# Attention scores as pairs of 64-row fp32 matmuls, reciprocals shared by two steps, and a new order

## The chip, the cores and the metric

The kernel runs on one core of one Trainium2 chip. The metric is device time in microseconds of one execution. The profile is that of one execution of the kernel before; all its times count from the start of its span.

## The reference

Attention over 4 batches of 8 heads, 576 tokens, 64 values a head. Only probabilities near the maximum are kept. Two feed-forward layers follow on 2304 tokens of 512 values, with 2048 hidden values each. Everything is float32.

```python
def _attn_ref(q, k, v, tau):
    scores = 1.0 / np.sqrt(q.shape[-1]) * np.matmul(q, k.transpose(0, 1, 3, 2))
    thresh = np.max(scores, axis=-1, keepdims=True) - tau
    scores = np.where(scores >= thresh, scores, -1000000000.0)
    attn = np.exp(scores - np.max(scores, axis=-1, keepdims=True))
    attn = attn / (np.sum(attn, axis=-1, keepdims=True) + 1e-09)
    return np.matmul(attn, v)

def _moe_ref(x, w_in, w_out):          # the second layer has max(0.01 * h, h) in place of g
    h = x @ w_in
    r = np.maximum(h, 0.0)
    g = r * r
    return g @ w_out
```

## The kernel before

**Attention.** The 32 heads are 16 pairs, four pairs to a batch, and each pair has nine steps (`steps`, `step`): four blocks of 128 query rows for each of its two heads, and one step of the 64 rows left over of both heads. 144 steps in all. A step computes 128 x 576 scores into the tile `s` (two PSUM banks of 288 columns each, index `g`; there are two such tiles), then on VectorE (DVE) the negated row maximum `nb` (L539), on ScalarE (ACT) `e`, the exponential (L540), a threshold `th` of 128x1 on DVE or GpSimd (POOL, L541 and L542), on DVE the masked `e` with its row sum (L544), then `t` and the reciprocal `r` of 128x1 (L547, L549). `e` times `r` is turned round and multiplied with the values.

**Two ways for the scores** (`prep` loads for one, `qk` at L529 multiplies). Pairs 0 to 5 (`nat`) keep queries and keys in fp32: the tile `Q` has one head's 64 rows and 64 rows of zeros, `KH` holds the keys of both heads one below the other, and each bank is one fp32 matmul over 128 rows. An fp32 matmul stands in the trace as two records. Pairs 6 to 15 split: queries and keys are rounded to fp32r on ACT, and the rests come from subtractions on POOL or DVE; `Q` holds the query's high part above its low part, `KH` and `KL` the two parts of the keys, and each bank takes two fp32r matmuls (`KH`, `KL`), the leftover step four. The leftover step of pairs 0 to 5 has products of 64 output columns that lie side by side in the array (the trace shows them as 128*64).

**Turning and values.** Pairs 0 to 4 (`nav`) turn `e` on TensorE (PE) through a unit matrix (L565, L566), copy it on ACT, and multiply in fp32 with 64 output columns at a time (`av32`, L631). Later pairs write `e` in two fp16 parts, turn them by DMA, and multiply in fp16 (L627); the last products of each group have 64 columns. `xs` adds the halves (L644 on DVE) and a DMA writes it to DRAM (`x1d`).

**Feed-forward.** While attention runs, the first layer works on the first 1792 tokens in seven blocks of 256, with 12 of the 16 weight blocks (`ffn`, `NFA`; h at L675, y at L701, all in fp32r parts, three products each). When attention is over, the other four weight blocks, the last 512 tokens and the second layer follow in blocks of 512 (h at L811, y at L857). Weights come as 512 KB loads that DVE, ACT and POOL unpack and split (`w_block`, L349 to L354).

**What sets the order.** `Plan.order` writes out every engine's order before the program is built: each operation has a priority (its step plus an offset from `CFG`), a cost, engines that may do it with a price for each, and tiles in rings of a fixed number of buffers. Engines then run their lists in that order, so a late instruction holds all behind it on its engine.

## Time and profile before

| | |
|---|---|
| time, median of 3 runs (lowest to highest) | 1092.0 us (1087.91 to 1092.18) |
| the profiled execution: time, and span of its trace | 1087.9 us, 1086.1 us |
| PE busy | 1059.4 us (98%) |
| DVE, ACT, POOL busy | 732.8 (67%), 509.1 (47%), 342.1 us (31%) |
| granted TensorE clock | full in each of 40 slices |
| HBM read and written | 70.98 and 17.83 MB |

The shares of the whole span mix three stages: attention alone at the start, attention with the first layer between its steps, and feed-forward alone at the end. Matmuls are pipelined, so that a PE that is busy throughout can still lose time between matmuls; starts of successive matmuls tell more than the busy time. POOL's times are rough.

### The profile page before, as it was taken

The page shows a single profiled execution, that of the slowest core. Times are in us where ns is not written, and L with a number is a line of the kernel's source. Part 1 is how long each engine was busy: PE and PEld are TensorE (multiplying, and loading weights), DVE is VectorE, ACT ScalarE, POOL GpSimd, SP SyncE. Part 2 cuts the span into 40 slices and gives each one's busy share as a digit, 9 for nine tenths or more (in the row PEclk, how much of TensorE's full clock was granted, in tenths as well). Part 3 has the DMA queues.
Part 4 walks back from the last instruction along what each step waited for, and adds up shares of the span by engine and source line. Part 5 has one row for each costly group of instructions (what it writes and reads, how often), then busy time and mean ns, then how long its engine had stood idle before and what let it go on. Part 6 is the DMA issues. An engine that isn't in the chain of part 4 may idle for free.

```text
span 1086.1 us, 17711 instructions
## 1 busy us (share of the span) xinstructions
PE 1059.4 (98%) x6343; PEld 886.1 (82%) x6343; DVE 732.8 (67%) x1557; ACT 509.1 (47%) x902; POOL 342.1 (31%) x421
## 2 busy tenths in 40 slices
PE   8988999999999999999999999999999999999998
PEld 4555778888998889989888888888888888888887
DVE  7999898788988898756999975763423433433343
ACT  6899878876776788735343431221211111111121
POOL 5765778889886676410000000000000000000000
PEclk9999999999999999999999999999999999999999
DMA  7444449998888896745644543610100100010010
GB/s 196 122 133 144 137 108 193 181 171 171 169 171 149 172 169 119 142 83 180 227 138 155 181 147 123 225 41 0 70 8 1 39 20 1 1 40 1 1 40 20
DMA packets 186983, 119.16 MB, mean 110 GB/s; under 512 B 146064, under 2 KB 164624, under 8 KB 186896
## 3 DMA queue, kind: packets, MB, share of 16 engines
q1 hardware_dynamic: 186528, 117.82, 44.3%
q8 instruction: 50, 0.82, 0.3%
q10 hardware_dynamic: 368, 0.21, 0.1%
q14 instruction: 37, 0.30, 0.1%
HBM read 70.98 MB, written 17.83 MB: 82 GB/s over the span
## 4 chain that ended last, share of the span: by engine, by line
PE 65%; DVE 1%; ACT 1%; issue 0%; POOL 0%; ACTq 0%; POOLq 0%; DVEq 0%
PE h L811 26%; PE y L857 26%; PE h L675 5%; PE y L701 5%; PE o L627 2%; PE s L529 2%; DVE e L544 0%; DVE nb L539 0%; DVE P L308 0%; ACT e L540 0%; ACT P L554 0%; DVE gl L308 0%; DVE P L587 0%; ACT tmp L639 0%; POOL t L547 0%
## 5 line engine op out<-in xcount | busy, mean ns | idle before, releaser
L823 DVE TENSOR_TENSOR r<-h,r 128x512 f32<-128x512 f32 (+1 forms) x80 | 51.0, 638 | 211.4 <-ACT r L822 211.4
L822 ACT ACTIVATE r<-h 128x512 f32<-128x512 f32 (+1 forms) x80 | 44.5, 557 | 313.1 <-PE h L811 310.6
L310 POOL TENSOR_TENSOR xl<-xr,xh 128x512 fp32r<-128x512 f32 (+1 forms) x11 | 12.7, 1157 | 418.3 <-ACT xh L297 253.5
L544 DVE SCALAR_TENSOR_TENSOR e<-s,th,e 128x576 f32<-128x576 f32 x144 | 116.8, 814 | 31.5 <-ACT e L540 27.4
L529 PE MATMUL s<-KH,Q 128*128 128x288 f32 (+1 forms) x440 | 121.1, 368 | 10.1 <-DVE e L544 6.6
L540 ACT ACTIVATE e<-s,nb 128x576 f32<-128x576 f32 x144 | 106.7, 742 | 38.5 <-DVE nb L539 22.5
L539 DVE TENSOR_REDUCE nb<-s 128x1 f32<-128x576 f32 x144 | 107.8, 750 | 12.4 <-PE s L529 11.3
L529 PEld LDWEIGHTS s<-KH,Q 128*128 128x128 f32 (+1 forms) x440 | 73.6, 183 | 30.6 <-issue 12.3
L308 DVE TENSOR_TENSOR gl<-r,gh 128x512 fp32r<-128x512 f32 (+1 forms) x129 | 85.6, 664 | 8.2
L587 DVE SCALAR_TENSOR_TENSOR P<-e,r,P 128x576 f16<-128x576 f32 x59 | 57.1, 970 | 2.8 <-ACT P L554 1.7
L819 ACT ACTIVATE r<-h 128x512 f32<-128x512 f32 (+1 forms) x32 | 18.2, 573 | 86.4 <-PE h L811 80.1
L627 PE MATMUL o<-PT,VA 128*128 128x320 f16 (+1 forms) x396 | 56.5, 287 | 0.4 <-DVE xs L644 0.4
L529 PE MATMUL s<-KL,Q 128*128 128x288 f32 x200 | 55.8, 294 | 0.0
L299 DVE CAST gh<-r 128x512 fp32r<-128x512 f32 (+1 forms) x103 | 43.8, 425 | 15.9 <-ACT r L684 7.8
L310 POOL TENSOR_TENSOR gl<-r,gh 128x512 fp32r<-128x512 f32 (+1 forms) x25 | 32.7, 1309 | 58.7 <-issue 45.2
L352 DVE SCALAR_TENSOR_TENSOR wraw<-wraw 128x512 int32<-128x512 int32 x64 | 48.9, 765 | 1.7 <-ACT wraw L349 0.6
L349 ACT ACTIVATE wraw<-wraw 128x512 f32<-128x512 f32 x64 | 43.0, 681 | 9.9 <-DMA wraw<-w 9.7
L354 DVE SCALAR_TENSOR_TENSOR wraw<-wraw 128x512 int32<-128x512 int32 x64 | 45.9, 717 | 0.6
L542 POOL TENSOR_SCALAR th<-nb,ca 128x1 f32<-128x1 f32 x75 | 33.3, 444 | 37.0 <-DVE nb L539 29.3
L627 PEld LDWEIGHTS <-VA 128*128 128x128 bf16 x396 | 35.2, 98 | 10.8 <-issue 0.4
L554 ACT ACTIVATE e<-e,r 128x576 f32<-128x576 f32 x51 | 39.4, 776 | 7.5 <-DVE r L549 6.9
L310 POOL TENSOR_TENSOR P<-e,P 128x576 f16<-128x576 f32 x29 | 38.7, 1339 | 8.5 <-ACT P L297 7.6
(616 smaller groups left out, 3044.5 us busy)
## 6 DMA issues: line engine op xcount, KB each, us to landing
wraw<-w SPq DMA_DIRECT2D x64, 512.0 KB, 4.1
wraw<-qT SPq DMA_DIRECT2D x20, 288.0 KB, 4.2
wraw<-kT SPq DMA_DIRECT2D x20, 288.0 KB, 4.4
out<-yo SPq DMA_DIRECT2D x18, 256.0 KB, 2.0
VA<-vv SPq DMA_DIRECT2D x32, 128.0 KB, 2.8
x2d<-yo SPq DMA_DIRECT2D x16, 256.0 KB, 3.3
xr<-x2d SPq DMA_DIRECT2D x4, 1024.0 KB, 5.8
y1d<-ys SPq DMA_DIRECT2D x14, 256.0 KB, 2.8
```

The lines of the kernel that those rows point to most:

```text
L308: alts.append(("V", dve(n), lambda: nc.vector.tensor_tensor(out=o(), in0=a(), in1=b(), op=alu), kind + "*"))
L310: alts.append(("G", pool2(n), lambda: nc.gpsimd.tensor_tensor(out=o(), in0=a(), in1=b(), op=alu), kind))
L529: nc.tensor.matmul(ps.get()[r, g, 0:S2], lhsT=o.Q.get()[:, q], rhs=(kk.get() if o.KL else f32(kk.get()))[:, g_(g)], start=k == 0 or not o. ...
L539: op(("V", 0.75, lambda: nc.vector.tensor_reduce(out=nb.get(), in_=pv(), axis=AX.XY, op=ALU.max, negate=True)), [ps], [nb], i + CFG["pd1"] ...
L540: op(("A", 0.74, lambda: nc.scalar.activation(e.get(), pv(), AF.Exp, bias=nb.get(), scale=1.0)), [ps, nb], [e], i + CFG["pex"], True)
L544: op(("V", 0.82, lambda: nc.vector.scalar_tensor_tensor(out=e.get(), in0=pv(), scalar=th.get(), in1=e.get(), op0=ALU.is_ge, op1=ALU.mult, ...
L587: op(("V", 0.8, lambda: nc.vector.scalar_tensor_tensor(out=lo(), in0=ev(), scalar=r_.get(), in1=hi(), op0=ALU.mult, op1=ALU.subtract), "*" ...
L627: nc.tensor.matmul(ps.get()[r, c_], lhsT=f_(v), rhs=parts16(pt)[:, j, c_], start=(k == 0), stop=k >= len(prods) - 2)
L675: nc.tensor.matmul(ps.get()[:, i], lhsT=a.get()[:, kc * P:(kc + 1) * P], rhs=x.get()[:, kc], start=(i == 0 and q == 0 and kc == 0), stop=( ...
L701: nc.tensor.matmul(yp[m // 2].get()[:, m % 2], lhsT=a.get()[:, c], rhs=x.get()[:, i], start=(f + i == 0 and q == 0 and m % 2 == 0), stop=( ...
L811: nc.tensor.matmul(ps.get()[:, 0:n], lhsT=a.get()[:, kc * P:(kc + 1) * P], rhs=x.get()[:, kc, 0:n], start=(q == 0 and kc == 0), stop=(q == ...
L857: nc.tensor.matmul(o(), lhsT=l, rhs=r, start=(first and q == 0), stop=(last and q == 2))
```

## The change

All 16 pairs compute their scores in one way. `Q` and `K` hold both heads' values in fp32 on partitions 0 to 63, and on partitions 64 to 127 the same queries again, with the other half of the keys' columns. A step is two fp32 matmuls over 64 rows each, one in the upper and one in the lower half of the array, each to a bank of its own; the leftover step has four of 64 rows and 64 columns. The splitting of queries and keys and the zero fill are gone. The heads of a pair take turns in the order of steps. The sums of two successive steps share one tile of two columns, with one `t` and one reciprocal for both; `th` is a subtraction. Some work may run on other engines (weights on POOL, two more `xs`), rings have other sizes, and all costs and offsets of the planner are new. Tokens 512 to 1023 do only 10 of the 12 weight blocks during attention (`nf`), and the two others afterwards.

```diff
-    lead1=1.311, xsg0=[1], lbm=8, lb=[[0, 1, 3, 4, 7], [0, 1, 3, 7], [3, 5], [2, 3, 5, 7]], xsm=4, xsg=[], dq=1.2, xu=False, pqk=-3.705,
...
+    hor=0.226, xlead=6.455, eb=5, pb=4, ptb=4, qb=2, nav=5, vb=2, tmb=1, gb=2, xb=1, w2step=-2.023, nf=[12, 10, 12, 12], wo=0.676, slack=0,
...
-    head, tail = [(0, 0), (0, 1), (1, 0), (1, 1)], [(0, 2), (0, 3), (None, MAIN), (1, 2), (1, 3)]
+    what = [(0, 0), (1, 0), (0, 1), (1, 1), (0, 2), (1, 2), (None, MAIN), (0, 3), (1, 3)]
...
+        Q, K = o.Q, o.K = [val("att", r, CFG["qb"], [P, 2, c], F32) for r, c in (("Q", S), ("K", S2))]
+        for g in range(2):
+            rows = slice(g * D, (g + 1) * D)
+            dma(lambda g=g, rows=rows: K.get()[rows], lambda g=g: kT[b, h0:h0 + 2, :, g * S2:(g + 1) * S2].rearrange("h d s -> d h s"), [], [K], at(0) if n else -3.1, D * S * 4, urgent=n == 0)
+            dma(lambda rows=rows: Q.get()[rows], lambda: qT[b, h0:h0 + 2].rearrange("h d s -> d h s"), [], [Q], at(0) if n else -3.05, 2 * D * S * 4, q=nc.sync if n else nc.scalar, urgent=n == 0, issue=0.5 if n else 0.06)
+        op(times(K.get, S)[0:None if n else 1], [K], [K], at(1))
...
+                    if h is None:
+                        a, q, r = j, slice((1 - j) * MAIN * P, (1 - j) * MAIN * P + REM), slice(j * REM, (j + 1) * REM)
+                    elif j == 0:
+                        a, q, r = h, slice(h * REM + t * P, h * REM + (t + 1) * P), slice(0, P)
...
+                    nc.tensor.matmul(ps.get()[r, g, 0:S2], lhsT=o.Q.get()[rows(g), a, q], rhs=o.K.get()[rows(g), a], start=True, stop=True)
...
+        k = i % 2
+        if not k:
+            sums[:] = [val("small", r, 3, [P, 2], F32) for r in ("sum", "t", "r")] + [Val(), Val()]
...
+        if k:
+            op([(g, c_, lambda eng=eng: eng.tensor_scalar(out=t_.get(), in0=sm.get(), scalar1=1e-9, scalar2=1.0 / UP, op0=ALU.add, op1=ALU.mult), "t")
+                for g, c_, eng in (("V", 0.148, nc.vector), ("G", 0.192, nc.gpsimd))], sums[0:1] + sums[3:], [t_], i + CFG["pd2"], True)
+            op(("V", 0.16, lambda: nc.vector.reciprocal(out=r_.get(), in_=t_.get())), [t_], [r_], i + CFG["pd2"], True)
```

Three places of the new order follow. In each row the line is that of its own kernel, then the operation, and the tiles (written <- read) with the size. The first place is PE in the middle of attention, between blocks of the first layer (h is L675 before and L635 now). Before:

```order
L675 MATMUL h<-xh,w8ih 128x256 x4
L675 MATMUL h<-xl,w8ih 128x256 x4
L675 MATMUL h<-xh,w8il 128x256 x4
L529 MATMUL s<-KH,Q_3644 128x288
L529 MATMUL s<-KL,Q_3644 128x288
L529 MATMUL s<-KH,Q_3644 128x288
L529 MATMUL s<-KL,Q_3644 128x288
```

Now:

```order
L635 MATMUL h<-xh,w8ih 128x256 x4
L635 MATMUL h<-xl,w8ih 128x256 x4
L635 MATMUL h<-xh,w8il 128x256 x4
L487 MATMUL s<-K,Q 128x288 x2
L635 MATMUL h<-xh,w9ih 128x256 x4
L635 MATMUL h<-xl,w9ih 128x256 x4
L635 MATMUL h<-xh,w9il 128x256 x4
L487 MATMUL s<-K,Q 128x288 x2
```

Four fp32r matmuls of 128 rows became two fp32 matmuls of 64 rows, between the same neighbours, which use all 128 rows.

The second place is DVE in the first stage, over some two steps. Before:

```order
L544 SCALAR_TENSOR_TENSOR e,sum<-s,th,e 128x576
L547 TENSOR_SCALAR t<-sum 128x1
L549 RECIPROCAL r<-t 128x1
L544 SCALAR_TENSOR_TENSOR e,sum<-s,th,e 128x576
L350 TENSOR_SCALAR wraw<-wraw 128x512
L352 SCALAR_TENSOR_TENSOR wraw<-wraw 128x512
L549 RECIPROCAL r<-t 128x1
```

Now:

```order
L494 TENSOR_TENSOR th<-ca,nb 128x1
L355 SCALAR_TENSOR_TENSOR wraw<-wraw 128x512
L500 SCALAR_TENSOR_TENSOR e,sum<-s,th,e 128x576 x2
L504 TENSOR_SCALAR t<-sum 128x2
L357 SCALAR_TENSOR_TENSOR wraw<-wraw 128x512
L506 RECIPROCAL r<-t 128x2
```

Two masked exponentials (L544, now L500) stand ahead of one reciprocal of 128x2, where each had one of 128x1.

The third place is POOL in the middle of attention, where it splits queries and keys. Before:

```order
L310 TENSOR_TENSOR KL<-wraw,KH 128x576
L547 TENSOR_SCALAR t<-sum 128x1
L553 TENSOR_SCALAR P_1_109<-e,r 128x576
L310 TENSOR_TENSOR gl<-r_3649,gh 128x512
L310 TENSOR_TENSOR VA<-VA 128x10x64
L310 TENSOR_TENSOR Q_3644<-wraw,Q_3644 64x576
L310 TENSOR_TENSOR gl<-r_3749,gh 128x512
```

Now:

```order
L513 TENSOR_SCALAR P_3_111<-e,r 128x576
L312 TENSOR_TENSOR P_2_110<-e,P_2_110 128x576
L312 TENSOR_TENSOR gl<-r_3556,gh 128x512
L494 TENSOR_TENSOR th<-ca,nb 128x1
L303 TENSOR_SCALAR P_1_109<-e 128x576
L494 TENSOR_TENSOR th<-ca,nb 128x1
```

The rows that write `KL` and `Q` are gone, and more of the probabilities' work (`P`) stands in their place.

## Rows read from the trace of the kernel before

**Rows 1.** Busy time of each engine by stage (instructions), clock, DMA share, GB/s

```profile
20.00:117.00 97.00, 85.58 (x477) 51.44 (x477) 87.83 (x210) 87.27 (x148) 67.51 (x102) 1.00 0.47 139
117.00:490.00 373.00, 366.03 (x2926) 325.70 (x2925) 310.41 (x725) 274.99 (x500) 261.36 (x294) 1.00 0.78 153
490.00:1086.00 596.00, 591.58 (x2873) 500.10 (x2872) 320.75 (x590) 134.91 (x239) 3.19 (x4) 1.00 0.23 75
```

**Rows 2.** Waits of PE, 117 to 490 us: total, times, longest

```profile
PE s L529 <- DVE e L544: 5.6, 9, 1.2
```

**Rows 3.** Timeline of PE at the first feed-forward matmul: start, length in us

```profile
117.31 0.72 PE L675 MATMUL h<-xh,w0ih 128*128 128x256 f32 x4
```

**Rows 4.** Timeline of PE, steps of an unsplit pair (two fp32 records each matmul)

```profile
21.48 2.14 PE L529 MATMUL s<-KH,Q 128*128 128x288 f32 x8
23.45 0.60 PE L565 MATMUL pt<-eye_sb,e 128*128 128x128 f32 x4
...
24.09 1.66 PE L631 MATMUL o<-PT,VA 128*64 128x256 f32 x10
25.68 1.24 PE L529 MATMUL s<-KH,Q 128*128 128x288 f32 x4
```

**Rows 5.** Timeline of PE, a step of a split pair between feed-forward matmuls

```profile
230.22 0.64 PE L675 MATMUL h<-xl,w9ih 128*128 128x256 f32 x4
230.70 0.64 PE L675 MATMUL h<-xh,w9il 128*128 128x256 f32 x4
231.17 0.30 PE L529 MATMUL s<-KH,Q 128*128 128x288 f32 x1
...
231.71 0.28 PE L701 MATMUL y<-gh,w6oh 128*128 128x256 f32 x1
```

**Rows 6.** Timeline of PE around a leftover step of 64-column products (pair 5)

```profile
159.12 0.28 PE L675 MATMUL h<-xh,w8ih 128*128 128x256 f32 x1
159.33 0.46 PE L529 MATMUL s<-KH,Q 128*64 128x288 f32 x2
...
160.11 0.41 PE L529 MATMUL s<-KH,Q 128*64 128x288 f32 x2
160.45 0.39 PE L675 MATMUL h<-xl,w8ih 128*128 128x256 f32 x1
```

**Rows 7.** Timeline of PE where 128*64 products turn to 64*64

```profile
15.33 0.39 PE L631 MATMUL o<-PT,VA 128*64 128x256 f32 x2
15.54 0.74 PE L631 MATMUL o<-PT,VA 128*64 128x256 f32 x3
15.86 0.43 PE L631 MATMUL o<-PT,VA 64*64 64x256 f32 x1
```

**Rows 8.** Groups of DVE, 0 to 116 us: busy us, mean ns, idle before

```profile
L544 DVE SCALAR_TENSOR_TENSOR e<-s,th,e 128x576 f32<-128x576 f32 x39 | 31.6, 814 | 3.7 <-ACT e L540 1.3 <-POOL t L547 1.0 <-POOL w7il L310 0.6
L539 DVE TENSOR_REDUCE nb<-s 128x1 f32<-128x576 f32 x40 | 30.0, 750 | 4.8 <-PE s L529 4.5
L352 DVE SCALAR_TENSOR_TENSOR wraw<-wraw 128x512 int32<-128x512 int32 x18 | 14.0, 777 | 0.2
L549 DVE RECIPROCAL r<-t 128x1 f32<-128x1 f32 x39 | 6.1, 156 | 0.9 <-POOL t L547 0.3
L541 DVE TENSOR_SCALAR th<-nb,ca 128x1 f32<-128x1 f32 x6 | 1.2, 208 | 0.1
```

**Rows 9.** Groups of ACT, 117 to 490 us, that split keys and queries

```profile
L297 ACT CAST KH<-wraw 128x576 fp32r<-128x576 f32 x19 | 12.7, 668 | 2.8 <-PE s L529 2.7
L297 ACT CAST Q<-wraw 128x576 fp32r<-128x576 f32 x19 | 12.4, 671 | 0.0
```

**Rows 10.** Groups of POOL, 117 to 490 us, that split keys and queries

```profile
L310 POOL TENSOR_TENSOR KL<-wraw,KH 128x576 fp32r<-128x576 f32 x18 | 27.3, 1518 | 4.0 <-ACT KH L297 3.7
L310 POOL TENSOR_TENSOR Q<-wraw,Q 64x576 fp32r<-64x576 f32 x17 | 27.0, 1594 | 2.0 <-DVE Q L299 0.8
```

**Rows 11.** DMA issues: count, KB each, median us from issue to landing

```profile
Q<-qT ACTq DMA_DIRECT2D x1, 144.0 KB, 3.8
wraw<-qT SPq DMA_DIRECT2D x20, 288.0 KB, 4.2
```

More of the change, by code (lines that the diff above doesn't have):

```diff
@@ L115, in ready @@
         def ready(o):
+            more = {}
             for v in o.news:
                 n = self.rings[v.ring]
-                if taken[v.ring] != v.k or (v.k >= n and any(x.start is None for x in seq[v.ring][v.k - n].ops)):
+                more[v.ring] = more.get(v.ring, 0) + 1
+                if taken[v.ring] + more[v.ring] - 1 != v.k or (v.k >= n and any(x.start is None for x in seq[v.ring][v.k - n].ops)):
                     return False
@@ L549, in step @@
-        op(("V", 0.158, lambda: nc.vector.reciprocal(out=r_.get(), in_=t_.get())), [t_], [r_], i + CFG["pd2"], True)
+        op([(g, c_, lambda eng=eng: eng.tensor_tensor(out=th.get(), in0=ca, in1=nb.get(), op=ALU.subtract), "th")
+            for g, c_, eng in (("V", 0.15, nc.vector), ("G", 0.22, nc.gpsimd))], [nb], [th], i + CFG["pd2"], True)
+        k = i % 2
+        if not k:
+            sums[:] = [val("small", r, 3, [P, 2], F32) for r in ("sum", "t", "r")] + [Val(), Val()]
+        sm, t_, r_ = sums[:3]
@@ L571, in step @@
                    [pt], [dst], i + CFG["pl"], True)
-            for key in [(n, 0, 1)] if h is None else [(n, h, t // 2)] if (h, t) in ((0, 1), (1, 1), (1, 3)) else []:
-                values(key, i)
+            if h is not None and t % 2:
+                values((n, h, t // 2), i)
             return
@@ L601, in step @@
             turn(chunk(n, h, cc), col * P, 0, P)
-            whole = [(n, h, cc)] if (h, t) in ((0, 1), (1, 1), (1, 3)) else []
-        for key in whole:
-            values(key, i)
+            if col:
+                values((n, h, cc), i)
     def values(key, i):
         n, h, c = key
-        b, p, _ = order[n]
+        b, p = order[n]
         o = pairs[n]
@@ L715, in ffn, with weights, clock @@
             dma(lambda m=m: y1d[j][2 * m * P:2 * (m + 1) * P, :].rearrange("(k p) t -> p k t", p=P), lambda ys=ys: ys.get(), [ys], [y1v[j]], pr, P * 2 * TA * 4)
-    avail = [(SPB * ((j * TA + TA - 1) // S + 1) if j or not CFG["two"] else begin[NP]) + CFG["xlead"] for j in range(NA)]
-    npieces = 5 * NFA // 2 + 2
-    per = npieces * (S / TA) / SPB * CFG["fend"]
+    avail = [SPB * ((j * TA + TA - 1) // S + 1) + CFG["xlead"] for j in range(NA)]
     now = [0.0]
-    for f in range(NFA):
-        W1[f] = w_block("wa", w1, f, f"w{f}", CFG["w0"] + CFG["wstep"] * f)
+    def weights(i):
+        while len(W1) < NFA and CFG["w0"] + CFG["wstep"] * len(W1) <= i:
+            f = len(W1)
+            W1[f] = w_block("wa", w1, f, f"w{f}", CFG["w0"] + CFG["wstep"] * f)
+    weights(CFG["w0"])
     prep(0)
     op(("S", 0.06, lambda: nc.scalar.dma_start(out=eye_sb, in_=eye)), [], [eye_v], -2.5, dma=move(P * P * 4))
-    jb = 0
-    def clock():
-        now[0] += 1.0 / per
+    def clock(nf):
+        now[0] += SPB / ((5 * nf // 2 + 2) * (S / TA) * CFG["fend"])
         return now[0]
-    oT = None
+    oT, rests = None, []
     for i in range(NS):
@@ L739, in tile_kernel @@
             oT = op(("N", 0.0, open1), [], [], i, after=[o for o in plan.ops if any(v.ring == "pt" for v in o.vals)])
+        weights(i)
         if i in begin and steps[i][0] + 1 < len(order):
             prep(steps[i][0] + 1)
-        step(i)
-        while jb < NA and avail[jb] <= i:
-            now[0] = max(now[0], avail[jb])
-            ffn(jb, clock)
-            jb += 1
+        rests.append(scores(i))
+        if i % 2:
+            for r in rests:
+                r()
+            rests = []
+    weights(10 * NS)
     att_ops = list(plan.ops)
-    while jb < NA:
-        now[0] = max(now[0], NS)
+    for jb in range(NA):
+        now[0] = max(now[0], min(avail[jb], NS))
         ffn(jb, clock)
-        jb += 1
     attn = [o for o in att_ops if any(v.ring in ATT for v in o.vals)]
```

162 lines of the change are left out of this document (53 added, 109 removed).

## The prediction

> **What bounds the kernel now.** I read the busy times by stage first, because the page's shares mix three stages. From 490 us on there is only feed-forward work, and PE is busy for 591.58 of 596 us, with no other engine above 54% [rows 1]. That stage has the same columns to multiply after the change. From 117 to 490 us attention and the first layer share PE: it is busy for 366.03 of 373 us, DVE for 310.41 (83%) [rows 1]. So PE is the bound there, and an instruction that goes from PE is worth its own time, because feed-forward matmuls stand ready behind it. The 7 us in which PE stands idle are mostly one wait, 5.6 us in 9 times: the next scores wait until DVE is done with the tile `s` [rows 2]. Before 117 us there is only attention, and the first feed-forward matmul starts at 117.31 us [rows 3]. In that stage PE is not full (85.58 of 97 us by busy times that overlap), and DVE and ACT are both near 90% (87.83 and 87.27) [rows 1]. So two sums are wanted: PE's work after the first feed-forward matmul, and the moment at which that one comes.
>
> **Scores on PE.** Three prices, each from start to start. Two steps of an unsplit pair (8 records) go from 21.48 to 23.45 us: 0.985 us a step, or 0.246 us a record [rows 4]. A step of a split pair goes from 231.17 to 231.71, 0.54 us; four matmuls of 0.133 make 0.53 [rows 5]. Its leftover step has eight, 1.07 us. Columns halved but side by side are shown by the leftover step of pair 5: two records at a time, and eight records in 160.45 - 159.33 = 1.12 us, where one after the other would take 8 x 0.246 = 1.97 [rows 4, 6]. So halves of the array do work at the same time when they lie side by side in columns. The new step has its halves one above the other, which no row shows. If they run together, a step streams for 2 x 0.246 = 0.492 us; if not, 0.985 us. I take 0.492, because the nearest rows are the column halves [rows 6].
>
> TensorE: Matmul & The Clock Gate of the Trainium skill, Part 3 on packing, says that row tiles run together too, and gives a further tile some 4 ns; by it a step would be an estimated 0.49 us, and by the other reading the sum below would rise by 50 us. No row here shows row tiles, and the sum rests on the column halves alone.
>
> By the new order the first feed-forward matmul comes after 42 steps instead of 40. Before, 104 steps lay behind it: 14 unsplit (13.8 us), 80 split (42.6), 10 split leftovers (10.7), together 67.1 us. Now 102 x 0.492 = 50.2. That is **-16.9 us**. One turning (0.55) and one product group of `av32` (25.68 - 24.09 = 1.59) [rows 4] also move ahead of it: **-2.1 us**. The two weight blocks that move to the last stage keep their columns, so they count as nothing; the cover is that PE is full in both stages.
>
> **Changes of the array's shape.** The same rows show what goes against the change. The last h matmul before the leftover step starts at 159.12, and 256 columns take 0.12 (0.48 for four, 230.22 to 230.70 [rows 5]), but the first score starts at 159.33: 0.09 us are lost when the array goes from 128x128 to 128x64, and again 0.10 when it goes back (160.11 to 160.45 for a record of 0.246) [rows 6]. The first records after each change are longer, too (0.46 instead of 0.41, 0.39 instead of 0.28): weights that were not loaded ahead, 0.05 and 0.10 us [rows 6]. Is it so for a change of rows alone? One place shows it: 128*64 records follow at 0.21 us, but the first 64*64 one starts 0.32 us after the last 128*64 one (15.86 - 15.54) [rows 7]. So yes, about 0.1.
>
> Counted in PE's orders from the first feed-forward matmul on, wherever an instruction's shape differs from that of its predecessor, there are 101 such changes before and 256 now, 155 more: most steps stand alone between full-size matmuls. At nothing each that adds 0, at the gap and the long loads (0.197 us) 30.5 us. I take the gap alone, 0.094 us, which every change in the rows has; the length of the loads differs with the shape, and the two halves of a step may load beside one another. That is **+14.6 us**.
>
> TensorEngine Tiling (Array Packing) of the Trainium skill, Key Properties, says that a change of the tiling mode drains TensorE. It names no price; it speaks against any count at nothing, and rows 7 agree with it at some 0.1 us.
>
> **The first stage.** Until the 40th score DVE's new order has 20 reciprocals fewer (-20 x 0.156 = -3.1 us), 11 more `th` (at most 11 x 0.208 = +2.3), and three weight parts fewer, which are unpacked later (three operations of at most 0.78 each, -7 us at most); two more steps cost 2 x (0.750 + 0.814) = +3.1 [rows 8]. That gives -4.7 us of some 117. ACT loses more, since POOL takes over scaling and unpacking; POOL has room (67.51 of 97 us [rows 1]). Pair 0's queries now come as 288 KB instead of 144 KB loads, 4.2 against 3.8 us to landing [rows 11]: +0.4. Unpacking that was put off could hold up the first weight blocks. I take **-3 us**, with ends of -7 and +2.
>
> **Relief of the other engines.** In the second stage ACT loses 25.1 us of casts [rows 9] and POOL 54.3 us of subtractions [rows 10], DVE about half of its reciprocals. The casts and subtractions themselves are worth nothing directly, as PE covers them. What they can give back is PE's idle time, 7 us at most and nothing at least. The wait on `s` hangs on DVE [rows 2], which loses least: **-4 us**. What is late next is the pair's shared reciprocal: the first step of each pair of steps keeps its `e` until the second one's sum is there. Five buffers of `e` instead of three cover that; without them DVE would stop once per two steps.
>
> **The sum.** -16.9 - 2.1 + 14.6 - 3 - 4 = -11.4 us. It is made against the profiled execution, whose span is 1086.1 us and whose time is 1087.9; the median of the three runs is 1092.0, and I put the difference there: 1092.0 - 11.4 = **1080.6 us**.
>
> **Rivals.** *The shape costs nothing.* If a change of rows alone does not stop the array, the 14.6 us fall away: 1066 us. For it: both halves have 128 columns like their neighbours, and rows 7 change from halves of columns, not from the whole array. Against it: the same gap of 0.09 to 0.11 us stands at every change that the rows have.
>
> *The shape costs all of it.* Gaps and long loads at 155 changes are 30.5 us instead of 14.6: 1096.5 us, no change that can be told. For it: rows 6 show both parts at one isolated step between h matmuls, which is just where the new steps stand. Against it: where steps or 64-column products stand next to one another, less is to be loaded anew.
>
> *The halves wait for each other* (slower than before). If the two 64-row products of a step run one after the other, 102 x 0.492 = 50.2 us come on top: 1131 us. It decides in every step, at the start of the second product: at about 0.01 us after the first one the forecast holds; from 0.24 us on, the length of one record, the gain is gone, since 102 x 0.246 = 25.1 us is twice the 11.4. For it: no row shows row halves together. Against it: column halves start together [rows 6].
>
> *The change isn't what it says,* in that an engine other than PE bounds the second stage: DVE would have to go from 83% to full [rows 1], while its list gets shorter. I give it no chance of its own.
>
> **How the numbers follow.** The forecast, with a cost of 0.06 to 0.13 us a change, has 0.43 and lies between 1074 and 1086. No cost for the shape: 0.22, 1060 to 1073. All of its cost: 0.24, 1087 to 1099. Halves one after the other: 0.08, at 1131; 0.03 are left for other losses above 1099. The ends of the first stage and of the relief (some 4 us each way) are in these stretches. A measurement of this kernel can tell about 0.5% from no change, so faster means below 1086.5: the first two, 0.65. The third lies within 0.5%, up to 1097.5, for 0.20 of its 0.24; the rest, 0.04 + 0.08 + 0.03 = 0.15, is slower. The range from 1061 to 1097 leaves out that rest and the lowest end of the second case, some 0.18 in all. The likeliest case alone has 1074 to 1086.
>
> **What would show it.** In the new trace: the starts of a step's two 64-row products (0.01 us apart, or more); the gap from the last h matmul to the first score beyond 0.12 us, and the one after the last record beyond 0.246; the start of the first feed-forward matmul (114 us, between 110 and 119); PE's idle time from there to the end of attention (3 us instead of 7). The prediction is wrong if a step takes less than 0.55 or more than 0.8 us of PE between feed-forward matmuls, or if the first feed-forward matmul comes after 120 us.

## The result, and the profile after

The changed kernel is slower, where I had forecast faster.

| | before | after |
|---|---|---|
| time, median (lowest to highest) | 1092.1 us (1087.91 to 1092.33) | 1104.3 us (1103.59 to 1104.72) |
| ratio, with its 95% interval | | 1.012 [1.0095, 1.0145] |
| profiled execution: time, span | 1087.9, 1086.1 us | 1104.7, 1102.8 us |
| first feed-forward matmul | 117.31 us | 130.57 us |
| from there to the end of the span | 968.8 us | 972.3 us |
| busy PE, DVE, ACT, POOL | 1059.4, 732.8, 509.1, 342.1 us | 1068.6, 742.6, 454.7, 288.3 us |

ACT and POOL are each busy 54 us less. On POOL that is as much as the subtractions of the splitting took [rows 10]; on ACT the casts were 25 us of it [rows 9], and 18 us are scalings of `e` that POOL does now. PE's busy time rose by 9 us and DVE's by 10, although 72 reciprocals are gone. The two spans differ by 16.7 us: 13.25 lie ahead of the first feed-forward matmul (the first h), 3.46 behind it. The medians differ by 12.2 only: the profiled execution of before lay 4.1 us below its median, that of after near its own. So up to some 4 us of a difference to the spans of before can be spread between executions.

Busy time of each engine by stage (sum, then PE, PEld, DVE, ACT and POOL, then granted clock, DMA share, GB/s), in the changed kernel:

```profile
20.00:130.00 110.00, 91.13 (x540) 47.34 (x538) 101.64 (x216) 77.41 (x130) 71.46 (x102) 0.95 0.48 132
130.00:490.00 360.00, 356.10 (x2756) 278.12 (x2755) 303.20 (x608) 235.34 (x445) 206.27 (x260) 1.00 0.78 151
490.00:1102.00 612.00, 608.48 (x2971) 514.33 (x2969) 328.40 (x601) 136.44 (x239) 6.78 (x6) 1.00 0.23 74
```

Against [rows 1], PE still bounds the second stage (all but 3.9 us of 360 are busy, where 7 of 373 were missing) and the third. The first stage is another one: DVE is now at 92% of it, ACT at 70%, and the granted clock is 0.95 in the mean.

Behind the first feed-forward matmul the question is what a step takes. Timeline of PE at a step that stands alone between feed-forward matmuls, changed kernel (start, length, us):

```profile
207.74 0.28 PE L635 MATMUL h<-xh,w3il 128*128 128x256 f32 x1
207.94 0.76 PE L487 MATMUL s<-K,Q 64*128 64x288 f32 x4
208.63 0.39 PE L661 MATMUL y<-gh,w0oh 128*128 128x256 f32 x1
208.85 0.28 PE L661 MATMUL y<-gl,w0oh 128*128 128x256 f32 x1
208.97 0.29 PE L661 MATMUL y<-gh,w0ol 128*128 128x256 f32 x1
```

A feed-forward record follows its predecessor at 0.12 us (208.85 to 208.97). The first score comes 0.20 us after the last h, so 0.09 is lost on the way in (to the ns: 207.735 and 207.944). The first y record starts at 208.63, 0.69 us after the first score, where two pairs side by side stream for 2 x 0.243 = 0.486; and the first y record takes 0.22 instead of 0.12 until the next. So the halves do run together (in each pair the starts are 7 ns apart), but the step costs PE 208.85 - 207.74 - 2 x 0.12 = 0.87 us. It's so everywhere: of 49 such steps the median is 0.878, and 43 are 0.878 or 0.879. The same measure gives 0.533 for the split steps of before. Each of the two changes of shape costs (0.878 - 0.486) / 2 = 0.196 us: 0.09 of it is the gap, and 0.10 a longer first record behind the change. That the longer record is a load of weights that did not run ahead is my reading; no run tests it.

TensorEngine Tiling (Array Packing) of the Trainium skill, Key Properties, says that a change of the tiling mode drains TensorE, without a price. The trace agrees with it in that time is lost at each change: 0.196 us, of which the gap is under half.

Ahead of the first feed-forward matmul, DVE's groups until 130 us (busy us, mean ns, idle before):

```profile
L500 DVE SCALAR_TENSOR_TENSOR e<-s,th,e 128x576 f32<-128x576 f32 x42 | 33.9, 810 | 1.9 <-ACT e L493 1.5
L492 DVE TENSOR_REDUCE nb<-s 128x1 f32<-128x576 f32 x42 | 31.1, 747 | 9.1 <-PE s L487 8.6
L494 DVE TENSOR_TENSOR th<-ca,nb 128x1 f32<-128x1 f32 x17 | 7.9, 469 | 0.3
L506 DVE RECIPROCAL r<-t 128x2 f32<-128x2 f32 x20 | 3.1, 153 | 0.1
L504 DVE TENSOR_SCALAR t<-sum 128x2 f32<-128x2 f32 x6 | 2.8, 463 | 0.1
```

Against [rows 8] the reciprocals fell from 6.1 to 3.1 us as forecast. But a threshold takes 469 ns in the mean where it took 208, so 17 cost 7.9 us instead of 1.2 for six. One single column minus another took between 0.13 and 2.44 us in this trace. Over the whole span 27 of the 72 thresholds on DVE started while POOL ran nothing: they took 0.13 to 0.16 us each. The other 45 started beside a running POOL instruction and took 0.59 us in the mean. And DVE waits 8.6 us for scores, where it waited 4.5 [rows 8].

PE at the start of the first stage, timeline of the changed kernel:

```profile
1.19 4.45 PE L406 MATMUL o<-P 128*128 128x512 f16 x10 [1.19 <-DVE P L403]
7.51 1.32 PE L487 MATMUL s<-K,Q 64*128 64x288 f32 x2 [1.88 <-DVE K L419]
...
20.05 1.11 PE L525 MATMUL pt<-eye_sb,e 128*128 128x128 f32 x4
...
29.42 0.66 PE L525 MATMUL pt<-eye_sb,e 128*128 128x128 f32 x4
```

After the ten warm-up matmuls PE stands idle for 1.88 us, as the keys come later than before (the first scores start at 7.51 us; before, at 5.44 without a gap). From then until some 28 us every record is longer: four turnings take 1.11 us where they take 0.60 [rows 4], a single one 417 ns instead of 273. That is the lower level of the clock (1.2 instead of 2.4 GHz): in e10 below, four turnings at 15.74 us take the same 1.11 us, and the clock column says 0.50 there. In this trace the column says 1.00.

But the late start is made good before the stage ends. The 40th row maximum, before and now (DVE):

```profile
115.31 0.76 DVE L539 TENSOR_REDUCE nb<-s 128x1 f32<-128x576 f32 x1 [0.40 <-PE s L529]
112.49 1.40 DVE L492 TENSOR_REDUCE nb<-s 128x1 f32<-128x576 f32 x2
```

The second row holds the 39th and the 40th, which starts at 113.2 us: 2.1 us earlier than before. From there to the first h it is 17.4 us, where it was 2.0. In this stretch of the changed kernel stand, by the timelines of POOL, DVE, ACT and PE:

```profile
118.64 0.98 POOL L504 TENSOR_SCALAR t<-sum 128x2 f32<-128x2 f32 x1 [1.37 <-DVE e L500]
119.82 0.14 DVE L506 RECIPROCAL r<-t 128x2 f32<-128x2 f32 x1
119.99 0.78 ACT L514 ACTIVATE e<-e,r 128x576 f32<-128x576 f32 x1 [0.92 <-DVE r L506]
120.82 1.12 PE L525 MATMUL s<-eye_sb,e 128*128 128x128 f32 x4 [4.64 <-ACT e L514]
```

PE stands idle for 4.64 us, its longest wait ahead of the first h (before, none was above 1.64 us). It waits for a scaled `e`, that for the reciprocal of two steps, and that for the second step's sum: the first `e` of the two was masked by 116.2 us, the second by 118.55, with a weight part of 1.70 us between them on DVE, and `t` took 0.98 us on POOL. Then PE's records are long again (four turnings 1.12 us), and the granted clock is 0.67 from 120 to 130 us. Two steps, a turning and a product group more lie ahead of the first h, too, as forecast.

### The profile page after: what moved, and what is told of

It is laid out like the page before. It is cut to its first block, busy times and chain, and to the rows that moved or that the text cites. A ratio compares the mean times of both kernels' runs of the same rounds, so it can differ in the third digit from the quotient of the medians.

```text
span 1102.8 us, 17365 instructions
## 1 busy us (share of the span) xinstructions
PE 1068.6 (97%) x6295; PEld 845.4 (77%) x6295; DVE 742.6 (67%) x1444; ACT 454.7 (41%) x821; POOL 288.3 (26%) x380
## 4 chain that ended last, share of the span: by engine, by line
PE 83%; DVE 6%; ACT 3%; issue 3%; DMA 2%; POOL 2%; SPq 1%; ACTq 0%; POOLq 0%; DVEq 0%
PE h L772 26%; PE y L818 26%; PE y L661 9%; PE h L635 8%; PE s L487 6%; PE o L585 4%; PE o L589 2%; DVE e L500 2%; DVE nb L492 2%; PE pt L525 1%; ACT e L493 1%; DMA K<-kT 1%; DMA Q<-qT 1%; POOL P L513 1%; DVE wraw L355 1%
## 5 line engine op out<-in xcount | busy, mean ns | idle before, releaser
L500 DVE SCALAR_TENSOR_TENSOR e<-s,th,e 128x576 f32<-128x576 f32 x144 | 116.2, 811 | 18.7 <-ACT e L493 16.7
L487 PE MATMUL s<-K,Q 64*128 64x288 f32 (+1 forms) x640 | 111.5, 464 | 13.2 <-DVE e L500 10.0
L487 PEld LDWEIGHTS s<-K,Q 64*128 64x128 f32 (+1 forms) x640 | 45.5, 181 | 43.4 <-issue 14.0
L301 DVE CAST gh<-r 128x512 fp32r<-128x512 f32 (+1 forms) x105 | 42.1, 401 | 16.7 <-ACT r L644 7.5
L513 POOL TENSOR_SCALAR e<-e,r 128x576 f32<-128x576 f32 x54 | 44.3, 825 | 16.4 <-DVE r L506 15.5
L589 PE MATMUL o<-PT,VA 128*64 128x256 f32 (+3 forms) x200 | 39.0, 446 | 3.7 <-DVE xs L602 1.9
L351 ACT ACTIVATE wraw<-wraw 128x512 f32<-128x512 f32 x50 | 33.8, 680 | 15.4 <-DMA wraw<-w 13.5
L312 POOL TENSOR_TENSOR P<-e,P 128x576 f16<-128x576 f32 x27 | 35.6, 1326 | 9.5 <-DVE P L301 6.6
L312 POOL TENSOR_TENSOR gl<-r,gh 128x512 fp32r<-128x512 f32 x24 | 34.7, 1446 | 11.3 <-ACT gh L299 11.3
L494 POOL TENSOR_TENSOR th<-ca,nb 128x1 f32<-128x1 f32 x72 | 22.7, 316 | 54.0 <-DVE nb L492 44.1
L597 ACT ACTIVATE tmp<-o 64x256 f32<-64x256 f32 (+1 forms) x64 | 26.1, 407 | 22.8 <-PE o L585 13.1
```

What stands on the lines that cost most here:

```text
L312: alts.append(("G", pool2(n), lambda: nc.gpsimd.tensor_tensor(out=o(), in0=a(), in1=b(), op=alu), kind))
L487: nc.tensor.matmul(ps.get()[r, g, 0:S2], lhsT=o.Q.get()[rows(g), a, q], rhs=o.K.get()[rows(g), a], start=True, stop=True)
L500: op(("V", 0.82, lambda: nc.vector.scalar_tensor_tensor(out=e.get(), in0=pv(), scalar=th.get(), in1=e.get(), op0=ALU.is_ge, op1=ALU.mult, ...
L589: nc.tensor.matmul(ps.get()[(lo3, up3)[j % 2], 0:w], lhsT=o.VA.get()[0:rows, j, h, 0], rhs=whole32(pt)[0:rows, j, 0:w], start=j < 2, stop= ...
```

## The experiments

The time from the first h on is counted to the end of the span in the table (972.3 us for the changed kernel, 968.8 before); the expectations count it to the last matmul (968.6 and 965.0). Both are of the profiled execution, the ratio is of medians. Steps are counted from 0.

| run | ratio to before, 95% | first h, us | rest of the span, us |
|---|---|---|---|
| the changed kernel | 1.012 [1.010, 1.015] | 130.6 | 972.3 |
| e1, the planner's old numbers | 1.019 [1.016, 1.023] | 125.4 | 986.2 |
| e2, the true price of a step | 1.027 [1.023, 1.032] | 131.7 | 985.5 |
| e3, e2 with two steps at once | 1.022 [1.019, 1.026] | 135.2 | 981.3 |
| e4, first loads by head | 1.011 [1.007, 1.015] | 127.4 | 975.8 |
| e5, first scores twice | 1.025 [1.022, 1.027] | 139.7 | 975.8 |
| e6, small operations in other forms | 1.013 [1.011, 1.015] | 126.2 | 975.2 |
| e7, e5 and e6 | 1.019 [1.017, 1.021] | 137.0 | 970.3 |
| e8, products over 128 rows | 1.039 [1.036, 1.041] | 138.0 | 992.2 |
| e9, before with halves in pairs 0 to 5 | 1.005 [1.003, 1.007] | 117.8 | 974.0 |
| e10, before with halves in all pairs | 1.010 [1.007, 1.014] | 122.5 | 977.9 |
| e11, before with shared reciprocals | 1.001 [0.999, 1.003] | 119.6 | 971.2 |
| e12, e9 and e11 | 1.006 [1.004, 1.008] | 122.3 | 973.4 |
| e13, e4 and e6 | 1.009 [1.006, 1.012] | 124.8 | 973.3 |
| e14, before with pair 5 split | 1.005 [1.003, 1.007] | 116.9 | 978.5 |

### Is it the planner? (e1 to e4)

The first idea was that the numbers of the planner, its 0.62 us for a step above all, were at fault.

e1 takes the offsets and prices of the planner of before, and 12 weight blocks throughout:

```diff
-    lead1=1.337, xsg0=[2], lbm=8, ...
+    lead1=1.311, xsg0=[1], lbm=8, ...
...
```

> The changed kernel with the planner's prices and offsets of the kernel before (rings, 64-row scores and shared reciprocals stay), and 12 weight blocks for all tokens. Theory A: two causes, the array's changes of shape (0.39 us for a step that stands alone) and an order that lets the first feed-forward matmul wait until 130.6 us instead of 117.3. By A the old numbers bring that matmul back to 114 to 121 us and the time to 1092 (1088 to 1097), while the work behind it stays some 968 us. Rival B: the first stage is late through what the change itself does (larger first loads, reciprocals that wait for a second step), whatever the order: still 127 us or later, and 1100 to 1106.

Measured: 1113.8 us, slower than the changed kernel, which neither theory said. The first h comes 5 us earlier, but 14 us are lost behind it; there are 283 changes of shape there instead of 256, and 5 us more of waiting.

e2 books what a step really takes:

```diff
-        op(("T", 0.62, qk), [o.Q, o.K], [ps], i + CFG["pqk"], True)
+        op(("T", 0.87, qk), [o.Q, o.K], [ps], i + CFG["pqk"], True)
```

> The changed kernel with one number of the planner changed: a step of scores is booked on TensorE with 0.87 us, as the trace of the change shows it between feed-forward matmuls, instead of 0.62. Theory A, in the form that the order was laid out for steps too cheap and its waits come from there: first feed-forward matmul at 115 to 122 us, time 1090 to 1097. Rival: the order's other offsets make the delay and the price does not matter: 128 us or later, 1101 to 1107.

Measured: 1121.9 us, the slowest of the orders and above both forecasts. Behind the first h PE's gaps of over 0.25 us between records add up to 13.6 us, where they were 3.7. The true price makes the written order worse, not better.

e3 saves changes of shape by doing two steps' scores in one go:

```diff
+        wide = 2 if i - i % 2 >= 44 else 1
...
+        if i % wide == 0:
+            two = [(*steps[i + d], both[d]) for d in range(wide)]
+            op(("T", 1.35 if wide == 2 else 0.87, lambda: [qk(*w) for w in two]), ...
```

> As e2_true_price, but from step 44 on TensorE computes the scores of two successive steps one right after the other, so that the array changes its shape for every second step only. Theory A (the changes of shape cost 0.39 us for each step that stands alone): some 50 round trips fewer are worth 15 to 20 us against e2_true_price, so 1073 to 1082, unless the two score tiles, which must both be free, add waits. Rival C: what is lost behind the first feed-forward matmul is not the shape: the same time as e2_true_price within 4 us.

Measured: 1117.3 us, 4.6 less than e2 where theory A said 15 to 20. Behind the first h it gains 4.2 us, though its gaps are longer (16.2 us by the same count), with 201 changes of shape where e2 has 254. Where two steps stand together between feed-forward matmuls, they cost 1.363 us (median of 23), which is 2 x 0.486 and the same two changes of 0.196. So the price holds for groups, too, and two steps together are still dearer than two split ones (2 x 0.533 = 1.066 us).

e4 brings pair 0's queries and keys head by head:

```diff
+        if not n:
+            for h in range(2):
+                for g in range(2):
...
+                    dma(lambda h=h, g=g, rows=rows: K.get()[rows, h], lambda h=h, g=g: kT[b, h0 + h, :, g * S2:(g + 1) * S2], ...
```

> The changed kernel, with the first pair's queries and keys loaded and scaled head by head, so that the first step needs 432 KB instead of 864 KB. First row maximum on VectorE at 7.5 to 9 us instead of 10.9. If the late start is on the path to the first feed-forward matmul, that one comes 2 to 4 us earlier and the time is 1100 to 1102. Rival: the stage has slack of its own later (the wait near 116 us), and the time stays at 1104 within 1.5 us.

Measured: the first maximum comes at 6.9 us instead of 10.9 and the first h at 127.4, 3.1 us earlier, but the time is 1104.1 us, the same, as the rival said: 3.6 us more behind it.

The first three say that the order matters by 10 us and more, and that a truer price does not mend it. e4 to e8 and e13 keep the order of all engines as it was; in e9 to e12 and e14 the planner made a new one.

### Price of the shape, clock, and small operations (e5 to e8)

e5 multiplies the first 42 steps' scores twice:

```diff
-            for j in range(2):
+            for j in list(range(2)) * (2 if i < 42 else 1):
```

> The changed kernel with the same order on every engine; only the scores of the first 42 steps (all before the first feed-forward matmul) are multiplied twice into the same tile, so that TensorE has as much to do per step there as it had before (0.98 instead of 0.49 us). Theory A (in the first stage TensorE has too little to do, its granted clock falls to the lower level in three stretches, and that is what makes the first feed-forward matmul late): the clock stays at 1.00 between 10 and 130 us, four turnings take 0.60 us throughout, the first feed-forward matmul comes at 118 to 124 us instead of 130.6, and the time is 1093 to 1099 us. Rival B (VectorE's list sets the first stage, and the fallen clock is only what a waiting TensorE shows): the first feed-forward matmul stays between 128 and 133 us, and the time between 1102 and 1107 us.

Theory A's forecast did not come. Clock by stretches (columns as above), and DVE's waits until 140 us (total, times, longest), both of e5:

```profile
10.00:20.00 10.00, 6.98 (x35) 4.54 (x35) 6.28 (x13) 3.50 (x6) 2.93 (x7) 1.00 0.99 210
...
30.00:110.00 80.00, 75.94 (x534) 43.58 (x531) 68.10 (x153) 51.87 (x87) 51.44 (x79) 1.00 0.41 111
...
120.00:130.00 10.00, 6.37 (x41) 3.04 (x37) 9.62 (x19) 6.92 (x13) 5.45 (x6) 1.00 0.58 177
130.00:140.00 10.00, 8.59 (x48) 5.30 (x49) 8.09 (x16) 6.80 (x13) 3.00 (x5) 0.83 0.61 154
```

```profile
DVE nb L492 <- PE s L487: 18.9, 27, 4.4
```

The clock column is full from 30 to 130 us, and yet the first h comes at 139.7 us, 9.2 later. DVE waits 18.9 us for scores instead of 8.6. So in this order the length of a score product lies on the chain of the first stage; rival B missed too, since DVE's list alone would have left the time as it was. What the lower clock costs isn't shown by this run: its cure and its price, products twice as long, came together.

e6 changes the forms of the small operations:

```diff
-eng.tensor_tensor(out=th.get(), in0=ca, in1=nb.get(), op=ALU.subtract)
+eng.tensor_scalar(out=th.get(), in0=nb.get(), scalar1=-1.0, scalar2=ca, op0=ALU.mult, op1=ALU.add)
...
+            cols = lambda eng: [slice(0, 1), slice(1, 2)] if eng is nc.vector else [slice(0, 2)]
```

> The changed kernel with the same order; only the small operations have another form: the threshold is again a multiply-add with a column as its operand, as in the kernel before (there 0.211 us in all 69 on VectorE), instead of the subtraction of two columns (72 on VectorE, mean 0.427, from 0.13 to 2.44 us in the trace of the changed kernel), and on VectorE the one t of 128x2 (35, mean 0.477, up to 1.57) is two of 128x1 (before 0.148 each). Theory B (VectorE's list sets the first stage, and the new forms wait there for POOL): until the first feed-forward matmul 17 thresholds save 4.4 us and 6 t some 1 us; it comes at 122 to 127 us instead of 130.6, and the time is 1096 to 1101 us. Theory A (the clock): VectorE's busy time falls by the same 5 us, but the first feed-forward matmul stays at 129 to 132 us and the time at 1103 to 1106 us.

The same groups of DVE, until 126 us, in e6 (t is L505 there, two rows of one column each time):

```profile
L494 DVE TENSOR_SCALAR th<-nb,ca 128x1 f32<-128x1 f32 x17 | 3.5, 212 | 0.4
L505 DVE TENSOR_SCALAR t<-sum 128x1 f32<-128x1 f32 x12 | 1.5, 149 | 0.0
```

In the same places between the same neighbours a threshold takes 212 ns instead of 469, and a t of two columns 2 x 149 instead of 463. DVE's busy time falls by 18 us in all (742.6 to 724.6), and the first h comes at 126.2 us, as theory B said. The time does not follow: 1103.9 us. At the scores of step 97 (315.9 us in the changed kernel) e6 is 7.3 us ahead of it, at those of step 109 (355.8 us) 0.8. e13 shows where that goes.

SBUF — State Buffer of the Trainium skill, the section on two separate sides, says that a VectorE instruction with two SBUF inputs (against a GpSimd one that reads SBUF), or in a 2-port mode, and a GpSimd instruction cannot use one pair of ports together: the one that starts first has it for its whole length. The trace agrees as to the forms: the threshold of two columns waits, the one with a column as its scalar does not (0.19 to 0.22 us in all 69 before).

e7 has both edits.

> Both edits at once: scores of the first 42 steps twice, and the small operations in the forms that do not wait. If both theories hold, the gains add up: first feed-forward matmul at 112 to 118 us, time 1086 to 1093 us. If only VectorE's list counts, it is as the kernel with the small forms alone, within 2 us; if only the clock counts, as the one with the doubled scores alone.

Measured: 137.0 us and 1110.9 us, between the two and none of the three forecasts. The small forms give 2.7 us at the first h, and the doubled scores cost 10.8.

e8 lets each product run over all 128 rows:

```diff
-        rows = lambda g: slice(g * D, (g + 1) * D)
+        rows = lambda g: slice(0, P)
```

> The changed kernel with the same order, but each score product runs over all 128 rows of the tiles (it sums the products of both halves of the keys, so the scores are other numbers); the two products of a step then follow one another (0.985 us of streaming instead of 0.492), and 161 of the 256 changes of shape behind the first feed-forward matmul are gone. The time from the first feed-forward matmul to the end was 968.6 us. If a change costs the gap and the long loads (some 0.197 us, 31 us for 161), it rises by 49.6 - 31.1 = 18 us to about 987; if a change costs the gap alone (0.094 us), by 35 to about 1003; if nothing, by 50. Before the first feed-forward matmul TensorE is busier, with no changes for the scores: by the theory of the clock it comes at 118 to 126 us (clock 1.00), by VectorE's list at 128 to 134 us.

The full price holds: to the last matmul 988.5 us, 19.9 more than the changed kernel, where the full price said 18 and the gap alone 35. By the records 109 changes of shape are left behind the first h instead of 256 (the leftover steps still change columns), so 147 fewer and not the 161 that I expected gave back 49.6 - 19.9 = 29.7 us, 0.20 each; 1.5 us of that is less waiting of PE. The first h, at 138.0 us, is later than both theories said; the products are twice as long there, as in e5. The timeline of PE at a step of e8:

```profile
181.84 0.28 PE L661 MATMUL y<-gh,w6ol 128*128 128x256 f32 x1
181.96 1.14 PE L487 MATMUL s<-K,Q 128*128 128x288 f32 x4
182.72 0.50 PE L661 MATMUL y<-gh,w6oh 128*128 128x256 f32 x1
183.05 0.28 PE L661 MATMUL y<-gl,w6oh 128*128 128x256 f32 x1
```

No gap ahead of the scores (0.12 us), so the gap belongs to the shape and not to the change from fp32r to fp32. The step costs 183.05 - 181.84 - 0.24 = 0.97 us; the median of 49 is 0.972. For a step alone between feed-forward matmuls this case has three prices: split 0.533, halves 0.878, unsplit 0.972. Halving the product halves its streaming and saves a tenth.

### One part at a time, in the kernel before (e9 to e12)

e9 and e10 put the 64-row products into the kernel before, for the unsplit pairs and for all:

```diff
+                for g in range(2):
+                    rows = slice(g * D, (g + 1) * D)
+                    nc.tensor.matmul(ps.get()[r, g, 0:S2], lhsT=o.Q3()[rows, hh, q], rhs=o.K3()[rows, hh], start=True, stop=True)
...
-    hor=-0.24, xlead=5.45, ..., nat=[0, 1, 2, 3, 4, 5], ...
+    hor=-0.24, xlead=5.45, ..., nat=[0, 1, 2, 3, 4, 5, 6, 7, 8, 9, 10, 11, 12, 13, 14, 15], ...
```

The last two lines are e10's alone.

> The kernel before with one part of the change: pairs 0 to 5, which it does not split, take their scores as two 64-row fp32 products side by side; pairs 6 to 15 stay split, reciprocals, thresholds and the planner's numbers stay. Theory (the first stage of the changed kernel is late through its order and its slow small operations, not through the scores): the first feed-forward matmul comes at 114 to 120 us (117.3 before), and the time is 1086 to 1093 us, no change that can be told; behind it 14 steps cost 0.87 instead of 0.985 us. Rival (the halved scores themselves: with less to do TensorE's clock falls in the first 30 us, and the first loads of 288 KB come later): first feed-forward matmul at 122 to 128 us and 1097 to 1103 us.

> The kernel before with the scores of all 16 pairs as 64-row products, and nothing else of the change (own reciprocals, thresholds in the old form, the planner's old numbers, 12 weight blocks throughout). Theory (a change of shape costs its 0.19 us; the first stage suffers from the other parts): behind the first feed-forward matmul the products of scores and their changes of shape cost some 9 to 12 us more than the split ones, of which some 5 come back as less idle time; the first feed-forward matmul at 114 to 120 us; 1093 to 1100 us. Rival (halved scores make the first stage late): first feed-forward matmul after 123 us, 1104 to 1110 us.

e9: the first h comes at 117.8 us, as forecast, but 5 us are lost behind it, and the ratio of 1.005 is just outside no change. That loss is as much as PE waits longer: its gaps of over 0.25 us behind the first h add up to 12.4 us, where they were 6.9 before. e10: 1.010, within reach of the whole change's 1.012. **The scores, with the order that the planner makes for them, give nearly all of the loss.** Behind the first h 9.1 us are lost, with less waiting than before (4.5 us of gaps), so the work itself costs some 11.5 more: as priced (9 to 12). Ahead of it 5.2 us are lost, more than the theory allowed and less than its rival wanted. The form of the scores can't be all of that: e9 multiplies the first 40 steps in the same form, with the same first loads, and has its first h only 0.5 us later than before. e9 and e10 differ there in the order; what in it costs the other 4.6 us was not traced.

e11 shares the reciprocals in the kernel before, e12 has e9's edit too:

```diff
+            op([(g, c_, lambda eng=eng: [eng.tensor_scalar(out=t_.get()[:, c], in0=sm.get()[:, c], ...) for c in cols(eng)], "t")
...
-        step(i)
+        rests.append(step(i))
```

> The kernel before with shared reciprocals alone (one t and one reciprocal for two steps, t on VectorE as two operations of one column, four buffers of e instead of three, which is what fits). VectorE loses 72 reciprocals (11 us), 20 of them ahead of the first feed-forward matmul (3.1 us). Theory (VectorE's list sets the first stage): 1086 to 1092 us, first feed-forward matmul 113 to 117 us. Rival (the first step of each two waits for the second, which makes the chain from scores to x longer): first feed-forward matmul at 120 to 126 us, 1094 to 1102 us.

> The kernel before with both: 64-row scores in pairs 0 to 5 and shared reciprocals. If both are harmless, 1083 to 1090 us, the candidate for a version that beats both kernels; if the shared reciprocals delay the first feed-forward matmul, 1094 to 1102 us like the kernel with them alone; if the halved scores do, likewise like theirs.

e11 makes no difference that can be told (1.001): DVE loses 72 reciprocals, but the first h comes 2.3 us later, not earlier. e12 is slower than the kernel before by 0.6%, so it doesn't beat it.

### What takes the gain back, and a last try (e13, e14)

> The changed kernel with two edits that were measured singly: the first pair's loads head by head (alone: first feed-forward matmul at 127.5 us instead of 130.6, time 1104.1) and the small operations in the forms that do not wait for POOL (alone: 126.3 us, time 1103.9). If the two parts of the delay are separate, the first feed-forward matmul comes at 121.5 to 124.5 us. Theory C (the 13 us before it cost their full length): time 1095 to 1099 us. Rival D (a gain in the first stage is lost again behind 300 us, where VectorE waits for POOL, as in each of the two kernels alone): 1101 to 1105 us.

The first h comes at 124.8 us: 5.8 of the 7.4 us that the two edits gave singly. The 40th maximum starts at 108.4 us, 4.8 earlier than in the changed kernel; PE's wait for a scaled `e` behind it is still 3.7 us. The time, 1102.1 us, is what rival D said. At step 97 the kernel is 9.1 us ahead of the changed one, at step 109 only 4.2. Timelines of e13 in that place, of DVE and of POOL:

```profile
317.24 0.33 DVE L503 TENSOR_SCALAR th<-nb,ca 128x1 f32<-128x1 f32 x2
317.49 6.40 DVE L557 SCALAR_TENSOR_TENSOR P<-e,r,P 128x576 f16<-128x576 f32 x1
323.81 0.81 DVE L509 SCALAR_TENSOR_TENSOR e<-s,th,e 128x576 f32<-128x576 f32 x1
```

```profile
317.64 1.28 POOL L312 TENSOR_TENSOR gl<-r,gh 128x512 fp32r<-128x512 f32 x1
318.88 1.26 POOL L312 TENSOR_TENSOR VA<-VA 128x640 f32<-128x640 f32 x1
320.09 0.74 POOL L610 TENSOR_TENSOR xs<-xs,tmp 64x256 f32<-64x256 f32 x1
320.79 1.28 POOL L312 TENSOR_TENSOR P<-e,P 128x576 f16<-128x576 f32 x1
322.02 1.25 POOL L312 TENSOR_TENSOR VB<-VA 128x640 bf16<-128x640 f32 x1
```

The row that writes `P`, 0.81 us by itself, lasts 6.40 us, until 323.89. The last of POOL's five ends at 322.02 + 1.25 = 323.27, so its own work fits only behind them. Behind it in DVE's list are the masked exponentials, and on those waits the next score. The timeline of PE there:

```profile
320.34 0.64 PE L645 MATMUL h<-xh,w3il 128*128 128x256 f32 x4
324.77 0.76 PE L496 MATMUL s<-K,Q 64*128 64x288 f32 x4 [3.79 <-DVE e L509]
325.46 0.42 PE L671 MATMUL y<-gh,w0oh 128*128 128x256 f32 x1
325.68 0.41 PE L671 MATMUL y<-gl,w0oh 128*128 128x256 f32 x1
```

PE stands idle for 3.79 us, and then the y records follow at 0.21 us instead of 0.12, until 328 us: the granted clock is 0.64 from 324.77 to 328, so it has fallen to its lower level for most of that, and what follows the stall runs longer, too. In the changed kernel two slow thresholds (2.51 us together, from 326.35) stand at this place, and when they have had their turn the same `P` row takes 0.81. e6 has a row of 6.51 us here as well, across six rows of POOL. So where the thresholds no longer wait, a longer row does, and PE with it.

SBUF — State Buffer of the Trainium skill, the summary of rules for kernel authors, says that the second of the two to issue waits until the first has finished. Here a POOL row was running when the DVE row started (it ended at 317.69 us), and DVE waited for five more behind that one.

e14 splits pair 5 as well, since the split step is the cheapest:

```diff
-    nat=[0, 1, 2, 3, 4, 5]
+    nat=[0, 1, 2, 3, 4]
```

> The kernel before with pair 5 split as well (pairs 0 to 4 unsplit instead of 0 to 5). An isolated step between feed-forward matmuls took 0.53 us split, 0.97 as 128 rows of fp32 and 0.88 as two 64-row halves, so nine steps less at 0.97 give 8 x 0.44 = 3.5 us, and their leftover step some 0.25. Theory (TensorE bounds the stage, the split form is the cheapest between feed-forward matmuls): 1085 to 1090 us against some 1091. Rival (the splitting of one more pair, 4 casts and 4 subtractions with two loads, falls into the first stage, which has DVE and ACT near 90%): first feed-forward matmul 2 to 5 us later, 1091 to 1097 us.

Measured: 1097.0 us. The theory missed, and of its rival only the time came (at the edge, 1097): the first h stays (116.9 us), and 9.7 us are lost behind it, of which up to some 4 may be the fast profiled execution of before. PE's waits there, 117 to 300 us:

```profile
PE s L529 <- DVE e L544: 8.8, 9, 2.3
```

That wait is 8.8 us where it was 5.6 over the whole stage [rows 2], and all of PE's gaps of over 0.25 us behind the first h add up to 17.2 us instead of 6.9. So the loss is waiting and not the price of a step. What makes the wait longer wasn't traced further. No kernel tried here beats the one before.

## Why the prediction was wrong

- *PE bounds the second stage; the halves run together; the scores stream for 0.492 us.* Right: 356.10 of 360 us busy, pairs 7 ns apart, 0.486 us.
- *Changes of shape: 155 x 0.094 = +14.6 us.* **This term was mis-sized.** A change costs 0.196 us at an isolated step, the same in e3's groups of two, and 0.20 in the mean of e8. The second rival had the right price, and gave the reason: the long first records belong to it wherever steps stand alone. I had [rows 6] with both parts in them and took the gap alone, since the two halves of a step "may load beside one another". They don't save anything by it: the first pair takes 0.10 us longer, as the full-size record behind them does. By 0.196 the term is 30.4 us, 15.8 more.
- *Relief of 4 us.* Near in size: PE's time not busy fell from 7 to 3.9 us, and its wait on `s` from 5.6 to 2.2 (130 to 490 us). That ACT's 25 and POOL's 54 us of casts and subtractions gave nothing else fits a PE that is busy for 99% of the stage; no run takes them out alone.
- *The first stage: -3 us.* **The other failed step:** it came out at +13.3. I took the first h to follow DVE's list. Up to the 40th maximum it did: 113.2 us, 2.1 earlier than before. With the old forms of the small operations and the loads by head (e13) it starts at 108.4, 6.9 earlier than before, near the 7.8 that my list gives without the two steps. So forms and loads cost 4.8 us there, and 5.8 at the first h; I had counted DVE's new rows with the durations of the old forms, and the loads at 0.4 us. Behind the 40th maximum I had counted 3.1 us for two steps, but the stretch to the first h grew by 15.4 us (17.4 instead of 2.0). I had named what stands there, the pair's shared reciprocal, and written that five buffers of `e` cover it; they don't: PE waits 4.64 us for it, and the clock falls behind that wait (0.67 from 120 to 130 us). The two steps and PE's work that the order puts there are in the 15.4, too. What each of these is worth was not tested one by one, so the cause of this part stays open between them.
- *The sum by spans.* Forecast 1086.1 - 11.4 = 1074.7, measured 1102.8: 28.1 us off. The first stage is 16.3 of it, the price of the shape 15.8, together 32.1; 4 us the other way are not traced, as much as executions of the kernel before differ.
- *The step from span to median.* I carried over the 4.1 us by which the profiled execution lay under its median. The changed kernel's profile lies within 0.4 us of its median, so the time is 23.7 us off, not 28.1.
- *What would show it.* Two of the signs that I named came: a step of more than 0.8 us between feed-forward matmuls, and the first h after 120 us.

## What to carry to other kernels

Price an array half by what stands around it: here two 64-row products save 0.49 us of streaming against unsplit fp32 and lose 0.39 us at their two edges, and four split full-size products are cheaper between full-size matmuls (0.533 against 0.878 us). By these prices, an estimate, a group would have to hold nine steps (9 x 0.486 + 0.39 = 4.77 us against 9 x 0.533 = 4.80) before halves beat the split form. An operation on a single column can take three times as long as one on 576 if its form has to wait for another engine (2.44 against 0.81 us): look at its longest time, not at the size of its operands. Follow the chain to the instruction that matters, not only the list of the busiest engine: here the list ran ahead and the first h came late. And measure one edit with the order of all engines held fixed; the orders of e1 to e3 moved the time by 9 to 18 us, where the whole change cost 12.

## What the runs showed of the hardware that was not expected

- A DVE row of 0.81 us lasted 6.40 us while POOL ran five rows back to back, and ended 0.62 us after the last of them (e13; 6.51 us across six rows in e6).
- After an idle time of 3.79 us PE ran at the lower clock, and 256 columns took 0.21 us instead of 0.12. From 7.5 to some 28 us the records of the changed kernel show the lower clock while the clock column says 1.00; in e10, with the same gap after the warm-up, the column says 0.50 from 10 to 20 us. Where the column and the records differ, the records tell.
- Two row halves start 7 ns apart, but each change between halves and the whole array costs 0.196 us, nearly as long as one record streams (0.243).
